# Spreading the routing pieces of a fused attention and mixture-of-experts kernel over three slots, with one-hots on GpSimd

## The chip, the cores and the metric

The kernel runs on one core of a Trainium2 chip. The time is that of one execution on the device, in microseconds (us); of several runs the median is given. Beside the runs there is one execution with the hardware profiler, whose span and instruction times the profile shows.

A core has five engines, each with its own queue of instructions, taken in order: TensorE (PE in the profile, with its weight loads as PEld), VectorE (DVE), ScalarE (ACT), GpSimd (POOL) and SyncE (SP, which here issues DMAs).

## The reference

```
scores = scale * q @ k.T              # 8 batches x 8 heads, 576 tokens, head_dim 64
scores masked in blocks of 64         # block_i >= block_j
x = softmax(scores) @ v               # -> x[b, s, 512]
logits = x @ w_gate                   # 8 experts
local_gate = sigmoid(x @ w_local)
for s:                                # within a batch
    fresh_e = argmax(logits[s])
    e = fresh_e if s == 0 or local_gate[s] < 0.5 else prev_e
    prev_e = e
    p = softmax(logits[s])
    out[s] = p[e] * (relu(x[s] @ w1[e]) @ w2[e])
```

So a token either takes the expert of its own largest logit or that of the token before it. The 4608 tokens are then sorted by expert into tiles of 128 rows, and each tile goes through the two matrices of one expert.

## The kernel before

The attention runs over 32 pairs of heads (`NPR`), in a loop over `it` from -2 to 31; one value of `it` is called a pass here. It is a pipeline by hand: in pass `it` the pair `a = it + 2` is transposed and begun, the pair `c = it + 1` gets its row maxima and its first scores, the pair `e = it` its last scores and its products with V (`av`), and the pair `x = it - 1` is written out as rows. The order of the instructions in each engine's queue is the order of the code (`manual_schedule`).

In one pass VectorE does, in this order: `norm` (L533, L534) of the pair before, the middle reduction to maxima (`mid_maxima`: L577, L581), the high reduction (`high_maxima`: the widest L577, then small copies and L599), the low reduction (`top(a, 2)`: L577, L579) and `norm_last` (L541 to L544). GpSimd does the exchange of maxima (L590 to L592) after the middle reduction and after the low one, the shift of the middle maxima (L599), casts of q and k (L992, L1032 to L1036), the clearing of corners (L651), the cast of x to bfloat16 (L505, in the last passes L510) and, in most passes, two loads of expert weights (L63), which it issues as DMAs. Score tiles in PSUM rotate over three buffers (`seg_tile`), so the scores of the high reduction reuse the buffer that the middle reduction has read. The gate's sums over four pairs (`gate_sums`, L732) come at the end of every fourth pass.

The tokens are routed in four groups of 9 columns of 128 tokens (`GC = 9`). The pieces of the routing of the first three groups are put into the passes by a table: `at(pass, slot, piece)` files a piece, and `run(pass, slot)` emits it at the named place of the pass. The slots that matter, in the order of a pass:

- start: after `norm`, ahead of the middle reduction
- mid: after the middle reduction and exchange, ahead of the last scores of `e` and the high reduction
- top, begin: after the high reduction
- turn: after the low exchange and the transposes of the gate's sums, ahead of the second weight load
- gap: behind that load, ahead of the last products `av(e, g1, 4)`, `av(e, g1, 3)` and of `norm_last`
- late: behind `norm_last`, ahead of the other products
- end, first: at the end of the pass

For group `g` the pieces begin in pass `i0` = 9, 17 and 26: `gate` (GpSimd, L159 to L163) and `fresh` in `i0`, `fresh_b` and the transposes `rows_ps` (L186) in `i0 + 1`, `scan_rows` (L192, L193) in `i0 + 2`, `carry` in `i0 + 3`, `scanned` and `chosen_ps` in `i0 + 4`, `chosen`, `ranks_ps` and the shares in `i0 + 5`, `ranks` and `ranks_all` in `i0 + 6`, `ranks_b` in `i0 + 7`, then `shares_b` (the share of a token as a sum of three bfloat16 parts) and `shares_out`, a DMA on SyncE. Two groups make the first 11 tiles of the expert stage; for these, `whole`, `whole_b`, `tile_experts`, `taken`, `taken_b`, `high` and `inverse` make the list of tokens, in passes 23 to 30. `low1(g, z)` makes the one-hots of the tokens' low rank bits, five or four columns of 128 at a time, in one VectorE instruction (L366); they are the left operand of `inverse`. In pass 30 the first rows are gathered. After pass 31 the expert stage runs over 36 tiles and more, with the fourth group's routing between them (`steps`).

Of the kernel before, what the change touches and what calls it, by code (L numbers as in the profile page):

```python
# [16 lines left out]
def kernel(  # L17
# [11 lines left out]
    nc = tc.nc  # L29
# [4 lines left out]
    AX = mybir.AxisListType.X  # L34
    AF = mybir.ActivationFunctionType
    ALU = mybir.AluOpType
# [6 lines left out]
    E = moe_w_gate.shape[1]  # L43
    F = moe_w1.shape[2]
    BS = B * S
    P = 128
# [24 lines left out]
    GC = BS // P // NG  # L71
# [8 lines left out]
    NTA = 2 * GC - E + 1  # L80
# [21 lines left out]
    desc_e = rt([P, E], F32, "desc_e")  # L102
# [4 lines left out]
    iota_lo = rt([P, P], BF16, "iota_lo")  # L107
# [11 lines left out]
    oh = rt([P, E, NC_], BF16, "oh")  # L119
# [35 lines left out]
    tmp = {}  # L155
# [9 lines left out]
    def fresh(g):  # L165

        lv = lg[:, :, :E]
        mx = sm9[:, 0, :]
        nc.vector.reduce_max(mx, lv, axis=AX)
        mxb = mx[:, :, None].to_broadcast([P, GC, E])  # L170
        nc.vector.tensor_tensor(tmp["eq"], lv, mxb, op=ALU.is_ge)
        nc.vector.tensor_sub(ep9, lv, mxb)
        nc.scalar.activation(ep9, ep9, func=AF.Exp)

    def fresh_b(g):
        best = sm9[:, 1, :]
        nc.vector.tensor_mul(tmp["eq"], tmp["eq"], desc_e[:, None, :].to_broadcast([P, GC, E]))
        nc.vector.reduce_max(best, tmp["eq"], axis=AX)
# [10 lines left out]
    def scan_rows(buf):  # L189

        s, kp = buf["sp"][:, 0, :], buf["sp"][:, 1, :]
        nc.vector.tensor_tensor_scan(s, kp, s, 0.0, op0=ALU.mult, op1=ALU.add)  # L192
        nc.vector.tensor_tensor_scan(buf["sp"][:, 1, :], kp, zeros, 1.0, op0=ALU.mult, op1=ALU.add)  # L193
        nc.vector.memset(buf["carry"][:, 0:1], 0.0)
# [35 lines left out]
    def ohg(g):  # L230
        return oh[:, :, GC * g:GC * g + GC]
# [30 lines left out]
    def ranks_all(g):  # L262
        off = sm9[:, 4, 0:E]
        nc.vector.tensor_add(tmp["pf"], tmp["pf"], off[:, :, None].to_broadcast([P, E, GC]))
        nc.vector.tensor_add(tmp["pf"], tmp["pf"], tots[:, 0, :].rearrange("p (e c) -> p e c", c=GC))
        nc.vector.tensor_mul(tmp["pf"], tmp["pf"], ohg(g))

    def ranks_b(g):
        rk = sm9[:, 5, :]
        nc.vector.reduce_sum(rk, over_e(tmp["pf"]), axis=AX)  # L270
        nc.vector.tensor_copy(ints[:, 0, 0, :], rk)
        nc.vector.tensor_single_scalar(ints[:, 1, 0, :], ints[:, 0, 0, :], 7,
                                       op=ALU.arith_shift_right)
        nc.vector.tensor_single_scalar(ints[:, 1, 1, :], ints[:, 0, 0, :], P - 1,
                                       op=ALU.bitwise_and)
        nc.vector.tensor_copy(hl[:, :, GC * g:GC * g + GC], ints[:, 1])
# [9 lines left out]
        nc.vector.reduce_sum(pg, ep9, axis=AX)  # L286
        nc.vector.tensor_mul(pgs, pg, sm)

    def shares_b(g):
        for j in range(3):  # L290
            nc.vector.tensor_copy(sh[:, :, j], pgs)
            if j < 2:
                nc.vector.tensor_sub(pgs, pgs, sh[:, :, j])

    def shares_out(g):
        nc.sync.dma_start(
            out=x_dram[GC * P * g:GC * P * g + GC * P, Dm:XW].rearrange("(c p) j -> p c j", p=P),
            in_=sh)

    def per_token(dst, w, n, tmp):  # L300

        nc.vector.tensor_mul(tmp, oh[:, :, 0:n], w[:, :, None].to_broadcast([P, E, n]))
        nc.vector.reduce_sum(dst, over_e(tmp), axis=AX)

    def shift7(dst, src, add):

# [120 lines left out]
    with tc.manual_schedule():  # L427
# [447 lines left out]
        def at(it, where, f):  # L875
            plan.setdefault((it, where), []).append(f)

        def low1(g, z):
            c0, n = GC * g + 5 * z, 5 - z
            low(ohl01[:, c0:c0 + n, :], c0, n)  # L880

        at(29, "first", lambda ps: inverse(ps, None, rhsa, na, NTA))
        for g in range(3):
            i0 = 8 * g + 9 + g // 2
            at(i0, "turn", lambda ps, g=g: gate(g))
            at(i0, "late" if g == 2 else "gap", lambda ps, g=g: fresh(g))
            at(i0 + 1, "gap", lambda ps, g=g: fresh_b(g))
            at(i0 + 1, "first", lambda ps: rows_ps(ps, buf))
            at(i0 + 2, "gap", lambda ps: scan_rows(buf))
            at(i0 + 2, "first", lambda ps: ends_ps(ps, buf))  # L890
            at(i0 + 2, "first", lambda ps: plan.update(ends=ends_in(ps)))
            at(i0 + 3, "gap", lambda ps: carry(plan["ends"], buf))
            at(i0 + 3, "first", lambda ps: carry_ps(ps, buf))
            at(i0 + 3, "first", lambda ps: carried(ps))
            at(i0 + 4, "gap", lambda ps: scanned(buf))
            at(i0 + 4, "first", lambda ps, g=g: chosen_ps(g, ps, buf))
            at(i0 + 4, "first", lambda ps: chosen_in(ps, nc.scalar.copy))
            at(i0 + 5, "start" if g == 2 else "gap", lambda ps, g=g: chosen(g))
            at(i0 + 5, "turned" if g == 2 else "first", lambda ps, g=g: ranks_ps(g, ps))
            at(i0 + 5, "turned" if g == 2 else "first", lambda ps: ranks_in(ps, nc.scalar.copy))  # L900
            if g == 2:
                at(i0 + 5, "gap", lambda ps, g=g: ranks(g))
                at(i0 + 5, "gap", lambda ps, g=g: ranks_all(g))
                at(i0 + 5, "end", lambda ps, g=g: ranks_b(g))
                break
            at(i0 + 5, "gap", lambda ps, g=g: shares_a(g))
            at(i0 + 5, "late", lambda ps, g=g: shares(g))
            at(i0 + 6, "gap", lambda ps, g=g: ranks(g))
            at(i0 + 6, "late", lambda ps, g=g: ranks_all(g))
            at(i0 + 7, "gap", lambda ps, g=g: ranks_b(g))  # L910
            at(i0 + 8 if g else i0 + 7, "late", lambda ps, g=g: shares_b(g))
            at(i0 + 9, "top", lambda ps, g=g: shares_out(g))
        at(17, "late", lambda ps: low1(0, 0))
        at(18, "late", lambda ps: low1(0, 1))
        at(23, "late", lambda ps: whole(False))
        at(24, "late", lambda ps: whole_b(NTA))
        at(25, "gap", lambda ps: tile_experts(tea, tend, NTA, tmpta))
        at(26, "gap", lambda ps: taken(t1ka, hia, na, tmpa))
        at(27, "late", lambda ps: taken_b(t1ka, hia, na))
        at(28, "turn", lambda ps: low1(1, 0))  # L920
        at(28, "late", lambda ps: high(ohha, rhsa, hia, 0, na, NTA))
        at(28, "late", lambda ps: high_b(ohha, rhsa))
        at(29, "gap", lambda ps: low1(1, 1))
        at(30, "start", lambda ps: inverse_in(plan["late"], inva, NTA))
        at(30, "mid", lambda ps: slots(inva, toka, None))
        for t in range(XGB):
# [312 lines left out]
        def highb():  # L1239
# [15 lines left out]
                 4: [lambda: shares_b(2), lambda: low2(0)],  # L1255
                 5: [lambda: shares_out(2), highb, lambda: gate(last), lambda: fresh(last)],
                 6: [lambda: inverse_in(cur[2], invb, NTB), lambda: slots(invb, tokb, None),
                     lambda: fresh_b(last)],
# [4 lines left out]
                 9: [lambda: chosen_in(cur[2], dve), lambda: chosen(last),  # L1263
                     lambda: new_g(1, lambda ps: ranks_ps(last, ps)),
                     lambda: ranks_in(cur[2], dve), lambda: ranks(last), lambda: ranks_all(last)],
                 10: [lambda: ranks_b(last), plan2],
# [93 lines left out]
```

## Time and profile before

| what | value |
|---|---|
| median of 3 runs | 458.43 us (458.36 to 460.65) |
| the profiled execution, its own time | 454.2 us |
| its span | 452.4 us |
| mean granted TensorE clock | 0.995 |
| TensorE busy | 432.8 us, 96% |
| VectorE busy | 315.1 us, 70% |
| GpSimd busy | 288.5 us, 64% |
| ScalarE busy | 273.6 us, 60% |

Busy time is the time in which an engine had an instruction in work. A row of a timeline gives the start, the length, the engine, the line of the kernel, the operation, what it writes and reads with shapes, a count, and in brackets the idle time before it with what ended that.

### The profile page before, as it was taken

What the parts mean: (1) busy time and instruction counts of PE and PEld (TensorE: products, weight loads), DVE (VectorE), ACT (ScalarE), POOL (GpSimd) and SP (SyncE); (2) the same over time, 40 slices, a digit from 0 to 9 for tenths busy, and PEclk for the clock granted to TensorE, in tenths of its full rate; (3) what the DMA queues carried; (4) which work ended last, traced back from release to release, by engine and by line L of the source; (5) the groups of instructions that cost most, each with busy time, mean ns of one, the idle gap of its engine ahead of it and who ended that gap; (6) DMA issues with size and microseconds to landing.
All of it is one profiled execution on the core that took longest, in us unless ns stands there. A gap on an engine that the chain in (4) does not pass through costs nothing.

```text
span 452.4 us, 19648 instructions
## 1 busy us (share of the span) xinstructions
PE 432.8 (96%) x7738; PEld 338.2 (75%) x7738; DVE 315.1 (70%) x856; ACT 273.6 (60%) x573; POOL 288.5 (64%) x674
## 2 busy tenths in 40 slices
PE   7899999999999999999999999987999999999994
PEld 5688787787788877787878777776676777777772
DVE  4777667768778888887788897954876884333422
ACT  3857766766667657665766666554454555555552
POOL 4556566667566747675556665672777758878853
PEclk8999999999999999999999999999999999999999
DMA  8999699999999975999779898887655665546532
GB/s 152 190 164 188 143 173 164 195 186 171 185 181 175 186 162 117 203 161 183 158 143 184 149 179 152 146 139 104 146 137 153 137 147 149 151 130 167 141 116 80
DMA packets 169885, 71.15 MB, mean 157 GB/s; under 512 B 151424, under 2 KB 158080, under 8 KB 169792
## 3 DMA queue, kind: packets, MB, share of 16 engines
q1 hardware_dynamic: 154640, 38.05, 44.5%
q0 software_dynamic: 13952, 31.52, 34.4%
q8 instruction: 64, 1.05, 1.0%
q10 hardware_dynamic: 1200, 0.30, 0.3%
q14 instruction: 29, 0.24, 0.2%
HBM read 67.18 MB, written 14.97 MB: 182 GB/s over the span
## 4 chain that ended last, share of the span: by engine, by line
PE 41%; DVE 26%; POOL 12%; issue 11%; DMA 5%; ACT 2%; POOLq 1%; DVEq 0%; ACTq 0%
PE g L667 10%; DVE mx L577 9%; PE ps_s L625 8%; POOL out_dram L822 6%; PE ps_s L634 4%; PE ps_h L798 4%; DMA out_dram<-o_sb,tok2s 3%; PE g L659 3%; PE ps_m L558 3%; PE ps_o L813 3%; PE g L951 2%; PE g L732 2%; DVE diag L599 2%; POOL diag L599 1%; DMA x_rows<-w_bf 1%
## 5 line engine op out<-in xcount | busy, mean ns | idle before, releaser
L641 ACT ACTIVATE prob<-ps_s 128x640 f32<-128x640 f32 (+2 forms) x128 | 103.6, 839 | 41.3 <-PE ps_s L634 40.4
L577 DVE TENSOR_REDUCE mx<-ps_m 128x2 f32<-128x640 f32 (+2 forms) x96 | 100.2, 1044 | 26.9 <-PE ps_m L558 19.9
L625 PE MATMUL ps_s<-plb 64*128 64x320 f32 (+4 forms) x768 | 107.3, 400 | 0.7 <-DVE mx L579 0.7
L625 PEld LDWEIGHTS ps_s<-plb 64*128 64x128 f32 x768 | 68.0, 189 | 20.8 <-issue 9.8
L667 PE MATMUL g<-vt,prob 128*64 128x65 f32 x2560 | 80.3, 222 | 0.0
L667 PEld LDWEIGHTS g<-vt,prob 128*64 128x64 f32 x2560 | 77.5, 138 | 0.1
L813 PE MATMUL ps_o<-w_bf,hT 128*128 x304 | 71.5, 380 | 0.0
L802 ACT ACTIVATE hT<-ps_h 128x512 bf16<-128x512 f32 x76 | 45.4, 597 | 26.6 <-PE ps_h L798 26.2
L816 ACT ACTIVATE o_sb<-ps_o,share 128x512 f32<-128x512 f32 x37 | 25.4, 686 | 40.2 <-PE ps_o L813 35.7
L813 PEld LDWEIGHTS <-hT 128*128 128x128 bf16 x304 | 28.0, 98 | 27.8 <-issue 0.3
L590 POOL COPY mx<-mx 64x2 f32<-64x2 f32 x64 | 11.7, 183 | 52.3 <-DVE mx L581 49.7
L779 DVE COPY natb<-w_bf 128x4096 bf16 x20 | 24.7, 1235 | 27.5 <-PE ps_h L798 25.2
L779 DVE COPY plb<-w_bf 128x4096 bf16 x20 | 25.1, 1253 | 24.6 <-PE ps_h L798 24.1
L798 PEld LDWEIGHTS <-plb 128*128 128x128 bf16 x608 | 35.4, 98 | 6.8 <-issue 2.9
L798 PEld LDWEIGHTS <-natb 128*128 128x128 bf16 x608 | 35.4, 98 | 6.2 <-DVE rs L541 1.5
L558 PE MATMUL ps_m<-kh,qh 64*128 64x320 bf16 (+3 forms) x256 | 37.6, 324 | 2.5 <-DVE mx L581 1.4
L634 PE MATMUL ps_s<-diag,ones 64*128 64x448 bf16 (+1 forms) x372 | 36.8, 274 | 2.0 <-DVE diag L599 0.4
L822 POOL DMA_INDIRECT out_dram<-o_sb,tok2s x17 | 28.7, 1690 | 11.6 <-ACT o_sb L816 7.0
L63 POOL DMA_DIRECT2D w_bf<-in_moe_w_dram x56 | 33.4, 596 | 1.4 <-DMA x_rows<-xb 0.4
L987 ACT COPY plb<-g 128x512 f32<-128x512 f32 x62 | 33.2, 593 | 0.3 <-PE g L951 0.2
L651 POOL MEMSET prob<- 64x128 f32 x128 | 24.5, 206 | 11.1 <-ACT prob L641 5.0
L798 PE MATMUL ps_h<-scr,plb 128*128 128x128 bf16 x416 | 25.3, 219 | 2.6 <-DVE share L788 2.3
(285 smaller groups left out, 769.8 us busy)
## 6 DMA issues: line engine op xcount, KB each, us to landing
w_bf<-in_moe_w_dram POOLq DMA_DIRECT2D x48, 256.0 KB, 4.5
vt<-in_v_dram SPq DMA_DIRECT2D x64, 128.0 KB
natb<-in_k_dram SPq DMA_DIRECT2D x63, 128.0 KB
natb<-in_q_dram SPq DMA_DIRECT2D x63, 128.0 KB
w_bf<-in_moe_w_dram POOLq DMA_DIRECT2D x8, 512.0 KB, 5.5
x_rows<-w_bf SPq DMA_DIRECT2D x13, 256.0 KB
natb<-in_k_dram SPq DMA_DIRECT2D x32, 32.0 KB
vt<-in_v_dram SPq DMA_DIRECT2D x32, 32.0 KB
```

The lines of the kernel that those rows point to most:

```text
L63: nc.gpsimd.dma_start(out=dst[:, e * WE:(e + 1) * WE].rearrange("p (k f) -> p k f", k=n)[:, r:r + m, :], in_=view[e][:, r:r + m, :])
L558: nc.tensor.matmul(ps[:, h, c:c + w], lhsT=qh[rows(h), 64 * b:64 * b + 128], rhs=kh[rows(h), 0:w], start=True, stop=m is None)
L577: nc.vector.reduce_max(mx[:, b:b + 2], ps[:, :, 0:w], axis=AX)
L625: nc.tensor.matmul(ps[:, h, c:c + n], lhsT=pls[i][rows(h), S + 128 * j:S + 128 * j + 128], rhs=pls[i][rows(h), a:a + n], start=part == 0, ...
L634: nc.tensor.matmul(ps[:, h, c:c + n], lhsT=ones[rows(h), :], rhs=diag[rows(h), a // 64:(a + n) // 64, :], start=False, stop=part == len(SE ...
L641: nc.scalar.activation(p[:, :, SEG0[s]:SEG0[s] + w], ps[:, :, 0:w], func=AF.Exp, scale=scale_attn)
L667: nc.tensor.matmul(g[rows(e), o + 65 * h:o + 65 * h + 65], lhsT=p[:, h, c:c + 64], rhs=t[:, j, h, :], start=(j == 0), stop=(j == m))
L779: nc.vector.tensor_copy(w, w1_bf[:, bass.ds(off, WE)])
L798: nc.tensor.matmul(ps_h[:, f, :], lhsT=w[:, f0 + ko * F:f0 + ko * F + 2 * P - 1:2], rhs=xb[:, ko * P:(ko + 1) * P], start=(ko == 0), stop= ...
L802: nc.scalar.activation(hT[:, half * 4:half * 4 + 4, :], ps_h, func=AF.Relu)
L813: nc.tensor.matmul(ps_o, lhsT=hT[:, fo, :], rhs=w2_bf[:, bass.ds(woff + fo * Dm, Dm)], start=(fo == 0), stop=(fo == FO - 1))
L822: wr = nc.gpsimd.indirect_dma_start(out=out_flat, out_offset=bass.IndirectOffsetOnAxis(ap=g[1][:, g[3]:g[3] + 1], axis=0), in_=o_sb, in_of ...
```

## The change

Pieces are cut in two and put elsewhere, and two kinds of work change the engine:

- `fresh_b` gives its first two instructions (L177, L178) to `fresh_a`, which goes to mid for the first two groups and to gap for the third. For the third group `fresh` goes from late to gap and `scan_rows` from gap to mid.
- `ranks_all` gives its last product (L266) to `ranks_own`, in mid of pass `i0 + 7`; `ranks_b` gives its first two instructions (L270, L271) to `ranks_a`, in gap; what is left of `ranks_b` goes to late, for group 1 one pass later than before.
- `shares_b` of the first two groups runs on GpSimd.
- `low1` runs on GpSimd, as one tensor_scalar for each column. For group 0 it stays late in passes 17 and 18; for group 1 it moves from turn of pass 28 and gap of pass 29 to late of passes 26 and 27.
- `whole` moves from late of pass 23 to gap of pass 24, `tile_experts` from gap to mid of pass 25. `taken` is cut into its two products (mid of passes 26 and 27) and its two reductions (late of the same passes); `taken_b` moves from late of pass 27 to gap of pass 28.
- In the expert stage the cut pieces run in the order that they had.

```
+    def fresh_a(g):
+        nc.vector.tensor_mul(tmp["eq"], tmp["eq"], desc_e[:, None, :].to_broadcast([P, GC, E]))
+        nc.vector.reduce_max(sm9[:, 1, :], tmp["eq"], axis=AX)
...
+    def ranks_own(g):
         nc.vector.tensor_mul(tmp["pf"], tmp["pf"], ohg(g))
 
-    def ranks_b(g):
+    def ranks_a(g):
         rk = sm9[:, 5, :]
         nc.vector.reduce_sum(rk, over_e(tmp["pf"]), axis=AX)
         nc.vector.tensor_copy(ints[:, 0, 0, :], rk)
+
+    def ranks_b(g):
...
-    def shares_b(g):
+    def shares_b(g, eng=nc.vector):
         for j in range(3):
-            nc.vector.tensor_copy(sh[:, :, j], pgs)
+            eng.tensor_copy(sh[:, :, j], pgs)
             if j < 2:
-                nc.vector.tensor_sub(pgs, pgs, sh[:, :, j])
+                eng.tensor_tensor(pgs, pgs, sh[:, :, j], op=ALU.subtract)
...
+    def per_token_a(w, n, tmp):
+        nc.vector.tensor_mul(tmp, oh[:, :, 0:n], w[:, :, None].to_broadcast([P, E, n]))
+
+    def per_token_b(dst, tmp):
+        nc.vector.reduce_sum(dst, over_e(tmp), axis=AX)
...
         def low1(g, z):
             c0, n = GC * g + 5 * z, 5 - z
-            low(ohl01[:, c0:c0 + n, :], c0, n)
+            for c in range(c0, c0 + n):
+                nc.gpsimd.tensor_scalar(ohl01[:, c, :], iota_lo, hl[:, 1, c:c + 1], 0.0,
+                                        op0=ALU.is_equal, op1=ALU.add)
...
-            at(i0, "late" if g == 2 else "gap", lambda ps, g=g: fresh(g))
+            at(i0, "gap", lambda ps, g=g: fresh(g))
+            at(i0 + 1, "gap" if g == 2 else "mid", lambda ps, g=g: fresh_a(g))
             at(i0 + 1, "gap", lambda ps, g=g: fresh_b(g))
             at(i0 + 1, "first", lambda ps: rows_ps(ps, buf))
-            at(i0 + 2, "gap", lambda ps: scan_rows(buf))
+            at(i0 + 2, "mid" if g == 2 else "gap", lambda ps: scan_rows(buf))
...
             at(i0 + 6, "late", lambda ps, g=g: ranks_all(g))
-            at(i0 + 7, "gap", lambda ps, g=g: ranks_b(g))
-            at(i0 + 8 if g else i0 + 7, "late", lambda ps, g=g: shares_b(g))
+            at(i0 + 7, "mid", lambda ps, g=g: ranks_own(g))
+            at(i0 + 8 if g else i0 + 7, "gap", lambda ps, g=g: ranks_a(g))
+            at(i0 + 8 if g else i0 + 7, "late", lambda ps, g=g: ranks_b(g))
+            at(i0 + 8 if g else i0 + 7, "late", lambda ps, g=g: shares_b(g, nc.gpsimd))
             at(i0 + 9, "top", lambda ps, g=g: shares_out(g))
         at(17, "late", lambda ps: low1(0, 0))
         at(18, "late", lambda ps: low1(0, 1))
-        at(23, "late", lambda ps: whole(False))
+        at(24, "gap", lambda ps: whole(False))
         at(24, "late", lambda ps: whole_b(NTA))
-        at(25, "gap", lambda ps: tile_experts(tea, tend, NTA, tmpta))
-        at(26, "gap", lambda ps: taken(t1ka, hia, na, tmpa))
-        at(27, "late", lambda ps: taken_b(t1ka, hia, na))
-        at(28, "turn", lambda ps: low1(1, 0))
+        at(25, "mid", lambda ps: tile_experts(tea, tend, NTA, tmpta))
+        at(26, "mid", lambda ps: per_token_a(t1, na, tmpa))
+        at(26, "late", lambda ps: per_token_b(t1ka, tmpa))
+        at(26, "late", lambda ps: low1(1, 0))
+        at(27, "mid", lambda ps: per_token_a(dd, na, tmpa))
+        at(27, "late", lambda ps: per_token_b(hia, tmpa))
+        at(27, "late", lambda ps: low1(1, 1))
+        at(28, "gap", lambda ps: taken_b(t1ka, hia, na))
         at(28, "late", lambda ps: high(ohha, rhsa, hia, 0, na, NTA))
         at(28, "late", lambda ps: high_b(ohha, rhsa))
-        at(29, "gap", lambda ps: low1(1, 1))
```

More of the change, by code (lines that the diff above doesn't have):

```diff
@@ L173, in fresh @@
         nc.scalar.activation(ep9, ep9, func=AF.Exp)
+    def fresh_a(g):
+        nc.vector.tensor_mul(tmp["eq"], tmp["eq"], desc_e[:, None, :].to_broadcast([P, GC, E]))
+        nc.vector.reduce_max(sm9[:, 1, :], tmp["eq"], axis=AX)
     def fresh_b(g):
         best = sm9[:, 1, :]
-        nc.vector.tensor_mul(tmp["eq"], tmp["eq"], desc_e[:, None, :].to_broadcast([P, GC, E]))
-        nc.vector.reduce_max(best, tmp["eq"], axis=AX)
         nc.vector.tensor_scalar(best, best, -1.0, float(E), op0=ALU.mult, op1=ALU.add)
@@ L298, in shares_out @@
             in_=sh)
+    def per_token_a(w, n, tmp):
+        nc.vector.tensor_mul(tmp, oh[:, :, 0:n], w[:, :, None].to_broadcast([P, E, n]))
+    def per_token_b(dst, tmp):
+        nc.vector.reduce_sum(dst, over_e(tmp), axis=AX)
     def per_token(dst, w, n, tmp):
-        nc.vector.tensor_mul(tmp, oh[:, :, 0:n], w[:, :, None].to_broadcast([P, E, n]))
-        nc.vector.reduce_sum(dst, over_e(tmp), axis=AX)
+        per_token_a(w, n, tmp)
+        per_token_b(dst, tmp)
     def shift7(dst, src, add):
@@ L903 @@
                 at(i0 + 5, "gap", lambda ps, g=g: ranks_all(g))
+                at(i0 + 5, "gap", lambda ps, g=g: ranks_own(g))
+                at(i0 + 5, "end", lambda ps, g=g: ranks_a(g))
                 at(i0 + 5, "end", lambda ps, g=g: ranks_b(g))
@@ L1257 @@
                  6: [lambda: inverse_in(cur[2], invb, NTB), lambda: slots(invb, tokb, None),
-                     lambda: fresh_b(last)],
+                     lambda: fresh_a(last), lambda: fresh_b(last)],
                  7: [lambda: scan_rows(buf)],
@@ L1264 @@
                      lambda: new_g(1, lambda ps: ranks_ps(last, ps)),
-                     lambda: ranks_in(cur[2], dve), lambda: ranks(last), lambda: ranks_all(last)],
-                 10: [lambda: ranks_b(last), plan2],
+                     lambda: ranks_in(cur[2], dve), lambda: ranks(last), lambda: ranks_all(last),
+                     lambda: ranks_own(last)],
+                 10: [lambda: ranks_a(last), lambda: ranks_b(last), plan2],
                  11: [plan2_a, lambda: plan2_b(tmp2, hi2)],
```

## The prediction

> **What bounds the kernel now.** I read the page first, then the chain of work that ended last, then the timelines of VectorE (DVE), GpSimd (POOL) and TensorE (PE), pass by pass. The page:
>
> ```profile
> span 452.4 us, 19648 instructions
> PE 432.8 (96%) x7738; PEld 338.2 (75%) x7738; DVE 315.1 (70%) x856; ACT 273.6 (60%) x573; POOL 288.5 (64%) x674
> PE 41%; DVE 26%; POOL 12%; issue 11%; DMA 5%; ACT 2%; POOLq 1%; DVEq 0%; ACTq 0%
> ```
>
> No engine bounds it alone: the chain changes hands inside each pass. Pass 7 holds no routing piece. Two pieces of its chain (start, length, what), then rows of the timelines of the three engines, picked out:
>
> ```profile
> 81.48 0.59 PE ps_s L634 x8
> ...
> 85.16 0.30 PE ps_m L558 x2
> ```
>
> ```profile
> 78.32 0.28 DVE L581 TENSOR_REDUCE mx<-ps_m 128x2 f32<-128x128 f32 x1
> 79.13 1.23 DVE L577 TENSOR_REDUCE mx<-ps_m 128x2 f32<-128x1024 f32 x1 [0.54 <-PE ps_m L558]
> 83.88 0.18 DVE L541 RECIPROCAL rs<-g 128x3 f32<-128x3 f32 x1 [1.11 <-PE g L667]
> 78.73 0.18 POOL L590 COPY mx<-mx 64x2 f32<-64x2 f32 x1 [1.40 <-DVE mx L581]
> 80.27 0.60 POOL L992 CAST qh<-plb 128x512 bf16<-128x512 f32 x1
> 80.98 0.30 PE L558 MATMUL ps_m<-kh,qh 64*128 64x320 bf16 x2
> ```
>
> I mark a pass by its widest reduction (L577 over 128x1024), which is always on the chain. From it to TensorE's L634 are 2.35 us (81.48 - 79.13), to the end of the last product with V 6.03 (85.16 - 79.13), and 2.57 more to the next mark, which stands at 87.73 (its row is the first below): a plain pass is 8.60 us.
>
> VectorE has idle time in two places: 0.54 us before the mark ("mid") and 1.11 before norm_last ("gap"). It has none after norm_last ("late"): the next instructions are L533 and L534, then the middle reduction, and TensorE's scores for the mark wait for that reduction to free their bank. GpSimd's exchange (L590) starts 0.13 us after the middle reduction; its chain ends with L992 at 80.87, 0.11 before the scores that read qh. So a delay of the middle reduction, or of GpSimd at that point, lengthens the pass almost at once.
>
> Where the routing lies, the marks are farther apart. The marks of passes 8, 9, 10 and 11, of 15 to 18, and of 23 to 29, each row alone out of VectorE's timeline:
>
> ```profile
> 87.73 1.23 DVE L577 TENSOR_REDUCE mx<-ps_m 128x2 f32<-128x1024 f32 x1 [0.54 <-PE ps_m L558]
> 97.54 1.23 DVE L577 TENSOR_REDUCE mx<-ps_m 128x2 f32<-128x1024 f32 x1 [0.85 <-PE ps_m L558]
> 106.13 1.23 DVE L577 TENSOR_REDUCE mx<-ps_m 128x2 f32<-128x1024 f32 x1 [0.53 <-PE ps_m L558]
> 115.48 1.23 DVE L577 TENSOR_REDUCE mx<-ps_m 128x2 f32<-128x1024 f32 x1 [0.85 <-PE ps_m L558]
> ```
>
> ```profile
> 151.85 1.23 DVE L577 TENSOR_REDUCE mx<-ps_m 128x2 f32<-128x1024 f32 x1 [0.67 <-PE ps_m L558]
> 160.97 1.23 DVE L577 TENSOR_REDUCE mx<-ps_m 128x2 f32<-128x1024 f32 x1 [0.49 <-PE ps_m L558]
> 170.79 1.23 DVE L577 TENSOR_REDUCE mx<-ps_m 128x2 f32<-128x1024 f32 x1 [0.85 <-PE ps_m L558]
> 179.70 1.23 DVE L577 TENSOR_REDUCE mx<-ps_m 128x2 f32<-128x1024 f32 x1 [0.49 <-PE ps_m L558]
> ```
>
> ```profile
> 224.77 1.23 DVE L577 TENSOR_REDUCE mx<-ps_m 128x2 f32<-128x1024 f32 x1 [0.71 <-PE ps_m L558]
> 234.36 1.23 DVE L577 TENSOR_REDUCE mx<-ps_m 128x2 f32<-128x1024 f32 x1 [0.49 <-PE ps_m L558]
> 244.45 1.23 DVE L577 TENSOR_REDUCE mx<-ps_m 128x2 f32<-128x1024 f32 x1 [0.85 <-PE ps_m L558]
> 253.88 1.23 DVE L577 TENSOR_REDUCE mx<-ps_m 128x2 f32<-128x1024 f32 x1 [0.49 <-PE ps_m L558]
> 262.98 1.23 DVE L577 TENSOR_REDUCE mx<-ps_m 128x2 f32<-128x1024 f32 x1 [0.49 <-PE ps_m L558]
> 271.92 1.23 DVE L577 TENSOR_REDUCE mx<-ps_m 128x2 f32<-128x1024 f32 x1 [0.49 <-PE ps_m L558]
> 282.50 1.23 DVE L577 TENSOR_REDUCE mx<-ps_m 128x2 f32<-128x1024 f32 x1 [0.85 <-PE ps_m L558]
> ```
>
> An idle time of 0.49 before a mark means that VectorE came last, since 0.49 is what TensorE takes after the middle reduction. A pass whose end holds gate_sums is 9.81 (87.73 to 97.54); every fourth is of that kind, 8, 16, 24 and 28 among those shown. Above 8.60 or 9.81 the passes that the change touches lose: pass 10 0.75, 15 0.52, 17 0.31, 23 0.99, 24 0.28, 25 0.83, 26 0.50, 27 0.34, 28 0.77. That is 5.29 us, and no more than that is to be had here. Pass 16 loses 0.01; in pass 18 I count no gain.
>
> **The change part by part.** The rows for the prices:
>
> ```profile
> 109.86 1.24 DVE L177 TENSOR_TENSOR scr<-scr,desc_e 128x72 f32<-128x72 f32 x1
> 110.28 0.72 POOL L505 CAST w_bf<-x 128x640 bf16<-128x640 f32 x1
> 185.72 0.32 PE g L186 x2
> 231.26 0.23 DVE L266 TENSOR_TENSOR scr<-scr,oh 128x72 f32<-128x72 f32 x1
> 231.41 0.17 DVE L308 TENSOR_SCALAR ints<-base 128x8 int32<-128x8 f32 x1
> 231.90 0.19 DVE L533 RECIPROCAL rs<-g 128x6 f32<-128x6 f32 x1
> 250.49 0.18 DVE L291 CAST sh<-pgs 128x9 bf16<-128x9 f32 x1
> 251.42 0.19 DVE L533 RECIPROCAL rs<-g 128x6 f32<-128x6 f32 x1
> 119.03 0.40 DVE L192 TENSOR_TENSOR_SCAN scr<-scr 9x128 f32<-9x128 f32 x1
> ```
>
> *Pass 10, fresh_a from gap to mid.* L177 took 1.24 us there, though its like (L266, same shape) takes 0.23: it ended 0.10 after GpSimd's cast L505 did, so it was held by that. In mid it and L178 (taken like L266) need some 0.5 us and have 0.53. The two instructions left in gap fit. Only the transposes of the next step stay on TensorE's path, 0.32: gain 0.75 - 0.32 = 0.43.
>
> *Pass 15, ranks_own out of late.* One L266 less, with its gap 0.26 us; it goes to mid of pass 16, where 0.49 are idle. Gain 0.26.
>
> *Pass 23, ranks_own and whole out of late.* From L308 to L533 were 0.49 us, L266 adds what remains from its start, 0.15: gain 0.64. They land in mid and gap of pass 24, the latter in place of ranks_b.
>
> *Pass 24.* ranks_b (five instructions, its second held by L505) leaves gap; three of whole come. whole_b stays in late, but norm_last is earlier, and gate_sums waited for it. This pass has the 1.21 us of gate_sums to hide whole_b. Gain 0.28.
>
> *Pass 25, late.* shares_b (0.93 us from 250.49 to 251.42) goes to GpSimd; three instructions of ranks_b, some 0.5 us, take its place, and tile_experts goes from gap to mid, where 0.85 are idle before 244.45. norm_last can then be about half a us earlier, as much as ranks_b needs. I take 0.78 of the 0.83.
>
> *Pass 27.* The reduction per_token_b replaces taken_b in late, but 0.32 of the loss of 0.34 is again the transposes: nothing.
>
> *Pass 28.* The first group's one-hots leave "turn", taken_b comes into gap, and two scans move from gap to mid. The scans need 0.40 each, 0.87 with what is around them; idle in mid are 0.49 and the 0.32 in which TensorE transposes. norm_last, for which gate_sums waited, is earlier: I take half of 0.77, 0.38, and 0 to 0.77 as bounds. The first scan also holds L590 up to 0.3 us, which is in these bounds.
>
> *Pass 29.* One one-hot piece leaves gap; the mark of pass 30 waits for other things by then: 0, at most +0.3.
>
> The sum of these is 0.43 + 0.26 + 0.64 + 0.28 + 0.78 + 0.38 = 2.77 us. The moved SP transfer, shares_out, keeps its pass; it waits for GpSimd's parts, finished more than half a pass before.
>
> *The one-hots on GpSimd* go the other way. Late in passes 17, 18, 26 and 27 come 5, 4, 5 and 4 tensor_scalar over 128x128, after the weight load in GpSimd's queue and ahead of the next exchange. In passes 17 and 26 the gate is in front of them too:
>
> ```profile
> 260.17 0.27 POOL L159 TENSOR_SCALAR ak<-lg 128x9 f32<-128x9 f32 x1
> 260.80 0.20 POOL L163 TENSOR_SCALAR sm<-ak 128x9 f32<-128x9 f32 x1
> 261.02 0.60 POOL L63 DMA_DIRECT2D w_bf<-in_moe_w_dram  x1
> L1036 POOL CAST qh<-plb 128x128 bf16<-128x128 f32 x31 | 9.1, 293 | 0.0
> ```
>
> GpSimd is free at 261.62. Undelayed, the next mark comes at 253.88 + 8.60 = 262.48, the exchange 0.40 before (79.13 - 78.73), at 262.08. To this I add a slack of 0.20, between 0.11 (80.87 to 80.98) and the 0.50 from 80.98 to L634. So 0.66 us are free. No row has this instruction at this size. Its nearest, L1036, is a one-input operation over 128x128 in 0.29; from below, 0.20 (L163, 128x9); from above, L159 compares 9 elements in 0.07 more than L163, which would be 1.0 us over 128 if it grew by element: 1.2. I take 0.30, by the nearest shape: five are 1.50, and the exchange is 0.84 late. Pass 17 then loses 0.84 instead of 0.31, pass 26 0.84 instead of 0.50: -0.87. Passes 18 and 27 have no gate (0.85 us, 260.17 to 261.02), so 1.51 are free and four cost 1.20: hidden; without that cover each would lose what passes 1.51. shares_b's five small steps (0.20 each, by L163) are hidden likewise in pass 25, and in pass 16.
>
> *Mid and GpSimd.* Eight steps in mid start 0.1 us before the exchange. The row of L177 shows that these two engines hold each other up. A step of 0.23 would hold L590 by about 0.1, inside the slack of 0.20: I count 0. [...]
>
> Net: 2.77 - 0.87 = 1.90 us. The profiled execution, 454.2 us with a span of 452.4, would take 452.3; the median of the runs shown, 458.43, lies 4.23 above it, and I take the same difference off: 456.5 us. From the bounds (one-hots at 0.25 to 0.40, where passes 18 and 27 lose 0.09 each too, and pass 28 from 0 to 0.77) this case alone reaches from 455.6 to 458.1.
>
> **The rivals.** *The one-hots fit.* If they cost 0.20 each, or the slack is nearer 0.50, passes 17 and 26 lose some 0.3 each instead of 0.81 together: gain 2.77 + 0.21 = 2.98, time 455.4. For it speaks the 0.20 of L163, where 119 more elements may add little; against it, the 0.29 of L1036 and the full queue of these two passes.
>
> *GpSimd becomes the bound (slower).* The place is the exchange after late in passes 17, 18, 26 and 27; the price is 5p - 0.66 twice and 4p - 1.51 twice for p us each. The old losses of 0.81 and the gains of 2.77 are used up at p = 0.44; from 0.56 on it is over 2.3 us slower. At 0.8 the time is 458.43 + 14.40 - 4.34 - 3.58 = 464.9. For it: L159's extra 0.07 for a compare of 9 elements. Against: L159 reads with a stride, and the 0.29 of L1036. [...]
>
> *Mid isn't free.* The exchange is held by each mid step for its whole length: six steps of 0.23 to 0.30 and the scans of 0.8, each less a slack of 0.11: 6 x 0.15 + 0.69 = 1.6 us are lost again. Time 458.1. For it: L177's row; against it: short steps and a start before the exchange.
>
> **How the numbers follow.** A difference of 0.5% (2.3 us) is about what a measurement of this kernel can tell from none. My forecast has 0.38, the fitting one-hots 0.30, the bound on GpSimd 0.22, mid not free 0.10. Forecast and last rival are within 0.5%: 0.48; faster 0.30; slower 0.22. The range goes from 454.8 (the fitting case with pass 28's whole 0.77 and 0.3 in pass 29) to 461.0, which takes in one-hots up to about 0.58; it leaves out the dearer ones.
>
> **What would show it.** In the changed profile the marks of passes 10, 23 and 25 should stand 8.9, 8.95 and 8.65 us before the next; L177 should take 0.23; the tensor_scalar of the one-hots some 0.30, with no idle time before L590 in the passes 18 and 27 that follow them. If passes 17 and 26 are 8.9 or less, the slack was larger; if they are over 10, GpSimd's compare is dear. The prediction is wrong if the marks outside passes 10 to 29 move, or if mid steps make VectorE come last where TensorE did.

## The result, and the profile after

The changed kernel takes 465.12 us (median of 8 runs, 462.45 to 467.25) against 459.32 us (8 runs, 456.35 to 460.65) for the kernel before beside it: ratio 1.0131, 95% interval 1.0101 to 1.0161. (Ratios, here and below, leave out runs over 1.5% above the fastest of the same kernel, and are not the quotients of the medians shown.) It is slower by 1.3%; forecast were 456.5 us and no more than 461.0. The profiled execution took 464.19 us.

Lines have moved in the changed kernel: the marks are L588 now, the middle reduction's end L592, the exchange L601, the cast of q L1013, the products with V L678; the one-hots on GpSimd are L892. The page's span, and in the same form as in the prediction the marks of passes 18 and 19, of 25, 26, 27 and 28:

```profile
span 462.5 us, 19661 instructions
```

```profile
180.59 1.23 DVE L588 TENSOR_REDUCE mx<-ps_m 128x2 f32<-128x1024 f32 x1
194.01 1.23 DVE L588 TENSOR_REDUCE mx<-ps_m 128x2 f32<-128x1024 f32 x1 [0.85 <-PE ps_m L569]
...
248.86 1.23 DVE L588 TENSOR_REDUCE mx<-ps_m 128x2 f32<-128x1024 f32 x1 [0.24 <-PE ps_m L569]
257.46 1.23 DVE L588 TENSOR_REDUCE mx<-ps_m 128x2 f32<-128x1024 f32 x1 [0.32 <-PE ps_m L569]
266.05 1.23 DVE L588 TENSOR_REDUCE mx<-ps_m 128x2 f32<-128x1024 f32 x1 [0.24 <-PE ps_m L569]
279.46 1.23 DVE L588 TENSOR_REDUCE mx<-ps_m 128x2 f32<-128x1024 f32 x1
```

Passes 25 and 26 are plain now: 8.60 and 8.59, where 9.43 and 9.10 were before. Passes 18 and 27 are 13.42 and 13.41, where 8.90 and 8.94 were. The marks by pass, in us to the next one:

| pass | before | forecast | after |
|---|---|---|---|
| 10 | 9.35 | 8.92 | 8.90 |
| 15 | 9.12 | 8.86 | 8.86 |
| 17 | 8.91 | 9.44 | 8.59 |
| 18 | 8.90 | 8.90 | 13.42 |
| 23 | 9.59 | 8.95 | 8.86 |
| 24 | 10.09 | 9.81 | 9.82 |
| 25 | 9.43 | 8.65 | 8.60 |
| 26 | 9.10 | 9.44 | 8.59 |
| 27 | 8.94 | 8.94 | 13.41 |
| 28 | 10.58 | 10.20 | 10.14 |
| 29 | 9.27 | 9.27 | 8.89 |

From the mark of pass 10 to that of pass 30 are 190.32 us (108.17 to 298.49) against 185.64 (106.13 to 291.77): 4.68 more, made of 8.99 lost in passes 18 and 27 and 4.3 gained in the others. So nearly all of the plan came true, and two passes took it back twice over. Of the 4.3, 0.2 is pass 13, which the change doesn't touch and which differs as much between profiles of one code.

What happens in one of the two, picked from the timelines of VectorE, GpSimd and TensorE:

```profile
179.15 0.60 POOL L63 DMA_DIRECT2D w_bf<-in_moe_w_dram  x1
179.78 0.28 DVE L592 TENSOR_REDUCE mx<-ps_m 128x2 f32<-128x128 f32 x1
179.80 3.52 POOL L892 TENSOR_SCALAR ohl<-iota_lo,hl 128x128 bf16<-128x128 bf16 x5
183.38 0.18 POOL L601 COPY mx<-mx 64x2 f32<-64x2 f32 x1
184.97 0.60 POOL L1013 CAST qh<-plb 128x512 bf16<-128x512 f32 x1
185.63 0.31 PE L569 MATMUL ps_m<-kh,qh 64*128 64x320 bf16 x2 [3.03 <-POOL qh L1013]
187.26 3.88 PE L678 MATMUL g<-vt,prob 128*64 128x65 f32 x80
```

The five one-hots of pass 17 take 3.52 us, 0.70 each. The middle reduction of pass 18 ends at 180.06, so the exchange could start 0.13 later, at 180.19; it starts at 183.38, 3.19 late. The cast of q ends at 185.57, and TensorE, which needs it, has stood for 3.03 us. What follows is a second loss: the 80 products with V take 3.88 us. In the same pass before they took 2.50:

```profile
183.22 2.50 PE L667 MATMUL g<-vt,prob 128*64 128x65 f32 x80
```

Pass 27 has a stall of 3.03 us too, and 3.77 us for the products. The clock granted to TensorE in pass 18, from the view of busy time by stretches (start and end, length, busy us and count of PE, PEld, DVE, ACT and POOL, then the granted clock; the last two columns are on DMAs and don't matter here):

```profile
184.00:185.60 1.60, 0.00 (x0) 0.00 (x0) 1.06 (x3) 0.04 (x1) 1.49 (x3) 1.00 1.34 167
185.60:186.50 0.90, 0.87 (x18) 0.56 (x20) 0.38 (x1) 0.10 (x1) 0.80 (x5) 1.00 1.20 126
186.50:187.50 1.00, 1.00 (x26) 1.00 (x28) 1.00 (x3) 1.00 (x2) 0.99 (x3) 0.65 0.36 52
187.50:188.50 1.00, 1.00 (x24) 1.00 (x22) 0.53 (x2) 0.74 (x1) 0.73 (x4) 0.50 0.54 68
188.50:189.50 1.00, 1.00 (x24) 1.00 (x22) 0.18 (x1) 0.00 (x0) 0.83 (x5) 0.50 1.04 181
189.50:190.50 1.00, 1.00 (x28) 1.00 (x26) 0.49 (x3) 0.00 (x0) 0.92 (x2) 0.64 0.91 256
190.50:191.50 1.00, 1.00 (x26) 0.71 (x24) 0.28 (x2) 0.01 (x1) 1.00 (x3) 1.00 0.94 133
```

Some 1.2 us after TensorE resumes at 185.63, the granted clock falls to 0.50, for some 3.4 us in which TensorE is busy all the time. Both times are estimates from the four stretches from 186.50 on (0.65 and 0.64 are means of stretches in which the clock changes).

### The profile page after: what moved, and what is told of

It reads as the page before. It is cut to its first block, busy times and chain, and to the rows that moved or that the text cites. A ratio compares the mean times of both kernels' runs of the same rounds, so it can differ in the third digit from the quotient of the medians.

```text
span 462.5 us, 19661 instructions
## 1 busy us (share of the span) xinstructions
PE 437.5 (95%) x7738; PEld 341.8 (74%) x7738; DVE 309.8 (67%) x842; ACT 271.4 (59%) x573; POOL 297.3 (64%) x702
## 4 chain that ended last, share of the span: by engine, by line
PE 62%; DVE 16%; POOL 6%; DMA 6%; issue 4%; ACT 3%; SPq 1%; another core or an unknown queue 1%; POOLq 0%; DVEq 0%; ACTq 0%
PE g L678 13%; PE ps_h L809 12%; PE ps_o L824 11%; PE ps_s L636 7%; DVE mx L588 6%; PE g L670 4%; PE ps_s L645 4%; PE ps_m L569 3%; DMA natb<-in_q_dram 2%; PE g L743 2%; PE g L972 2%; DMA x_rows<-w_bf 2%; DMA vt<-in_v_dram 2%; ACT prob L652 2%; POOL ohl L892 1%
## 5 line engine op out<-in xcount | busy, mean ns | idle before, releaser
L588 DVE TENSOR_REDUCE mx<-ps_m 128x2 f32<-128x640 f32 (+2 forms) x96 | 100.2, 1044 | 26.1 <-PE ps_m L569 16.7
L636 PE MATMUL ps_s<-plb 64*128 64x320 f32 (+4 forms) x768 | 106.1, 397 | 1.3 <-DVE mx L590 0.9
L678 PE MATMUL g<-vt,prob 128*64 128x65 f32 x2560 | 84.0, 226 | 0.5 <-issue 0.4
L678 PEld LDWEIGHTS g<-vt,prob 128*64 128x64 f32 x2560 | 80.8, 142 | 1.0 <-issue 0.9
L813 ACT ACTIVATE hT<-ps_h 128x512 bf16<-128x512 f32 x76 | 44.1, 597 | 47.7 <-PE ps_h L809 25.9
L601 POOL COPY mx<-mx 64x2 f32<-64x2 f32 x64 | 11.8, 185 | 43.4 <-DVE mx L592 37.1
L833 POOL DMA_INDIRECT out_dram<-o_sb,tok2s x17 | 21.6, 1270 | 18.4 <-ACT o_sb L827 9.5
```

Of the source, the lines that this page charges most:

```text
L588: nc.vector.reduce_max(mx[:, b:b + 2], ps[:, :, 0:w], axis=AX)
L636: nc.tensor.matmul(ps[:, h, c:c + n], lhsT=pls[i][rows(h), S + 128 * j:S + 128 * j + 128], rhs=pls[i][rows(h), a:a + n], start=part == 0, ...
L678: nc.tensor.matmul(g[rows(e), o + 65 * h:o + 65 * h + 65], lhsT=p[:, h, c:c + 64], rhs=t[:, j, h, :], start=(j == 0), stop=(j == m))
L813: nc.scalar.activation(hT[:, half * 4:half * 4 + 4, :], ps_h, func=AF.Relu)
```

## The experiments

My theory from here on (A): the one-hots on GpSimd cost all of the loss, by the late exchange and by the lower clock that follows the stall, and the rest of the change gains. Its rival (B): the steps in mid, and those that VectorE takes while GpSimd works, cost a part, so that the change is no faster without the one-hots.

**One-hots back on VectorE, all else as changed.**

```
-            for c in range(c0, c0 + n):
-                nc.gpsimd.tensor_scalar(ohl01[:, c, :], iota_lo, hl[:, 1, c:c + 1], 0.0, ...)
+            low(ohl01[:, c0:c0 + n, :], c0, n)
...
-        at(26, "late", lambda ps: low1(1, 0))
-        at(27, "late", lambda ps: low1(1, 1))
+        at(28, "turn", lambda ps: low1(1, 0))
+        at(29, "gap", lambda ps: low1(1, 1))
```

> The changed kernel with the one-hots of the first two groups on VectorE again, in the slots that they had before; all else as changed. Theory A (the one-hots on GpSimd cost all of the loss, by a late exchange, a stall of TensorE and a lower clock after it; the rest of the change gains): about 2.8 us less than before, some 456.5 against 459.3, passes 18 and 27 back to about 8.9. [...]

Measured: 453.82 us (10 runs) against 456.77 for the kernel before; ratio 0.9921, interval 0.9884 to 0.9958. The marks of pass 18 and 19:

```profile
183.94 1.23 DVE L588 TENSOR_REDUCE mx<-ps_m 128x2 f32<-128x1024 f32 x1
192.85 1.23 DVE L588 TENSOR_REDUCE mx<-ps_m 128x2 f32<-128x1024 f32 x1 [0.83 <-PE ps_m L569]
```

Pass 18 is 8.91 again, and passes 10 to 29 together are 182.91 us, 2.73 less than before. The expectation was 2.8. B has fallen: without the one-hots the change is faster than the kernel before. Whether mid costs a part is asked again below.

**One-hots on GpSimd alone, in the kernel before.**

```
-            low(ohl01[:, c0:c0 + n, :], c0, n)
+            for c in range(c0, c0 + n):
+                nc.gpsimd.tensor_scalar(ohl01[:, c, :], iota_lo, hl[:, 1, c:c + 1], 0.0, ...)
```

(and the same two pieces from passes 28 and 29 to late of 26 and 27)

> The kernel before with one part of the change alone: the one-hots as single instructions on GpSimd, late in passes 17, 18, 26 and 27. Theory A: about 8 us slower than before (two passes longer by 4.5 us each, less about 1 us that VectorE saves in passes 17, 28 and 29), ratio about 1.017, more than the whole change. Theory B: less than the whole change, under 1.010.

Measured: 462.89 us, ratio 1.0154 (1.0058 to 1.0251; 4 runs). Passes 10 to 29 take 192.02 us, 6.4 more than before, more than in the whole change (4.7) as A has it; but under the 8 expected, as pass 18 was only 11.80. The times alone can't tell 1.0154 from the whole change's 1.0131; this rests on the marks. Both stalls of this profile, and the clock after each:

```profile
186.30 0.31 PE L558 MATMUL ps_m<-kh,qh 64*128 64x320 bf16 x2 [2.98 <-POOL qh L994]
...
272.61 0.31 PE L558 MATMUL ps_m<-kh,qh 64*128 64x320 bf16 x2 [2.62 <-POOL qh L994]
```

```profile
188.00:189.00 1.00, 1.00 (x42) 1.00 (x38) 0.93 (x4) 0.91 (x2) 0.72 (x3) 1.00 0.55 70
...
274.50:275.50 1.00, 1.00 (x24) 1.00 (x22) 0.90 (x4) 0.72 (x1) 0.68 (x4) 0.50 0.74 101
```

A stall of 2.98 us left the clock at 1.00, one of 2.62 us halved it. In the first the products with V took 2.50 us, in the second 3.80. So the length of the stall alone doesn't decide.

**Three one-hots a pass**, in passes 17 to 19 and 26 to 28.

```
-            c0, n = GC * g + 5 * z, 5 - z
+            c0, n = GC * g + 3 * z, 3
...
+        at(19, "late", lambda ps: low1(0, 2))
+        at(28, "late", lambda ps: low1(1, 2))
```

> The changed kernel with three one-hots a pass in passes 17, 18, 19, 26, 27 and 28 instead of five and four. The exchange after passes 17 and 26 would be about 1.8 us late instead of 3.2, and TensorE would stand about 1.6 us instead of 3.0. If the lower clock comes only after a long stall (theory A1): TensorE's products with V take 2.33 us again and passes 18 and 27 are about 10.7 long; about 5.5 us less than the changed kernel, ratio to before 1.000. If any stall lowers the clock (A2): passes 18 and 27 about 12 us, ratio about 1.007.

Measured: 455.63 us, ratio 0.9947 (0.9903 to 0.9991). Passes 18 and 27 are 10.42 and 10.43. The stall and the products behind it:

```profile
186.13 0.31 PE L569 MATMUL ps_m<-kh,qh 64*128 64x320 bf16 x2 [1.61 <-POOL qh L1015]
...
187.55 2.50 PE L678 MATMUL g<-vt,prob 128*64 128x65 f32 x80
```

Half the stall, and the products take 2.50 us in this view, not 3.88; both stalls are 1.61 and neither lowers the clock (it stands at 1.00 in each stretch from 186.1 to 193.0). That is A1, for these two stalls. By the marks the kernel is level with before (185.59 us for passes 10 to 29, with 0.7 in pass 25 from a pause of TensorE that the experiment on the spread one-hots describes); the losses of 1.5 each in passes 18 and 27 eat most of the other gains. So the 0.5% by which its ratio is below 1.000 is more than the marks explain.

**The price of the one-hot by itself.** Sixteen more instructions on GpSimd ahead of the first pass:

```
+        for _ in range(2):
+            g.tensor_scalar(o1, iota_lo, n1, 0.0, op0=ALU.is_equal, op1=ALU.add)
+            g.tensor_scalar(o1, iota_lo, 5.0, 0.0, op0=ALU.is_equal, op1=ALU.add)
+            g.tensor_scalar(o1, iota_lo, n1, 0.0, op0=ALU.mult, op1=ALU.add)
+            g.tensor_scalar(o1, iota_lo, 5.0, 0.0, op0=ALU.mult, op1=ALU.add)
+            ... # the first and third in float32, then the first over 64 and 8 columns
```

> The kernel before with sixteen extra GpSimd instructions ahead of the first pass, whose results are overwritten later: tensor_scalar over 128 columns, compare or multiply, with the per-partition scalar or a constant, bfloat16 or float32, and the compare over 64 and 8 columns, each twice. The one-hot took 0.71 us in the changed kernel. If the compare is dear, the multiply takes 0.3 and the compare 0.7 in both types; if the scalar operand is dear, the constant takes 0.3; if bfloat16 is dear, float32 takes 0.3; if all tensor_scalar cost by element alike, all take 0.7 over 128, 0.45 over 64 and 0.2 over 8.

GpSimd's timeline in the one run of it, the second round:

```profile
7.68 0.71 POOL L859 TENSOR_SCALAR ohl<-iota_lo,nth 128x128 bf16<-128x128 bf16 x1
8.48 0.64 POOL L860 TENSOR_SCALAR ohl<-iota_lo 128x128 bf16<-128x128 bf16 x1
9.22 0.37 POOL L861 TENSOR_SCALAR ohl<-iota_lo,nth 128x128 bf16<-128x128 bf16 x1
9.68 0.30 POOL L862 TENSOR_SCALAR ohl<-iota_lo 128x128 bf16<-128x128 bf16 x1
10.05 0.71 POOL L863 TENSOR_SCALAR lgS<-id_f,nth 128x128 f32<-128x128 f32 x1
10.86 0.37 POOL L864 TENSOR_SCALAR lgS<-id_f,nth 128x128 f32<-128x128 f32 x1
11.20 0.50 POOL L865 TENSOR_SCALAR ohl<-iota_lo,nth 128x64 bf16<-128x64 bf16 x1
11.80 0.33 POOL L866 TENSOR_SCALAR ohl<-iota_lo,nth 128x8 bf16<-128x8 bf16 x1
```

The compare is what is dear: 0.71 against 0.37 for the multiply with the same operands. The scalar operand costs 0.07 of it (0.71 to 0.64, 0.37 to 0.30), the type nothing (float32 took 0.71 and 0.37 too). The compare grows by 3.2 ns a column ((0.71 - 0.33) / 120).

**TensorE kept busy through the stall.**

```
+            if job == 2 and i in (20, 29):
+                for _ in range(44):
+                    nc.tensor.matmul(ps[:, 0, 0:P], lhsT=ones, rhs=ones, start=True, stop=True)
             scores(ps, b, 0, w, m)
```

(`i` is the pair of heads: 20 and 29 are reached in passes 18 and 27.)

> The changed kernel with 44 extra small products on TensorE in passes 18 and 27, right before the scores that wait for the late cast; what they write is overwritten by these scores. They fill most of the stall and take nothing from the chain. Theory A1 (4.5 us a pass are 2.9 us of waiting and 1.5 us of products at a lower clock, which comes from the idle stretch): the clock stays at 1.0, the products with V take 2.33 us instead of 3.66, passes 18 and 27 are about 12.0 instead of 13.4; some 3 us less than the changed kernel. Rival (the low clock comes from what runs then, not from idleness): still 13.4.

Measured: 464.72 us against 460.21, ratio 1.0076 (1.0037 to 1.0115). The extra products (41 of the 44 stand in this row), the scores behind them, and the products with V (L681 here):

```profile
183.81 2.45 PE L579 MATMUL ps_m<-ones 128*128 128x128 bf16 x41
...
186.71 0.31 PE L569 MATMUL ps_m<-kh,qh 64*128 64x320 bf16 x2 [0.45 <-POOL qh L1016]
...
188.13 2.50 PE L681 MATMUL g<-vt,prob 128*64 128x65 f32 x80
```

```profile
188.00:190.50 2.50, 2.50 (x92) 2.50 (x86) 1.78 (x7) 1.31 (x2) 2.05 (x9) 1.00 0.89 117
```

The clock stays at 1.00 in both passes, and passes 18 and 27 are 11.83 and 11.84, by 44 products that do nothing for the result. This divides the loss: of the 4.5 us in each pass 2.92 are waiting (11.83 - 8.91) and 1.59 the clock (13.42 - 11.83). The same products run here at a clock of 1.00: the rival, that they bring the low clock, has fallen in these passes, and I put the low clock down to the idle stretch. The evidence is both filled stalls with the clock kept, against three of four unfilled ones of 2.6 to 3.0 us with it lost. Passes 19 and 28 are 9.25 and 10.74 here, 0.5 and 0.6 longer than in the changed kernel: the four one-hots that follow cost something once TensorE isn't slowed beside them. Altogether passes 10 to 29 are 188.53 us, 1.8 less than in the changed kernel and not the 3 expected.

**The shares' parts back on VectorE too** (first experiment's kernel, `shares_b(g)` for `shares_b(g, nc.gpsimd)`).

> The changed kernel with the one-hots and also the shares' parts (shares_b) on VectorE, as the first experiment but for the latter. Theory A: the pass in whose late slot they stand grows, as 0.9 us then lies behind 0.5 us of ranks_b: pass 25 from 8.60 to about 9.4, pass 16 unchanged since gate_sums covers it. Rival (GpSimd gains nothing there): pass 25 stays at 8.60.

One run. The marks of passes 25 and 26:

```profile
244.99 1.23 DVE L588 TENSOR_REDUCE mx<-ps_m 128x2 f32<-128x1024 f32 x1 [0.24 <-PE ps_m L569]
254.27 1.23 DVE L588 TENSOR_REDUCE mx<-ps_m 128x2 f32<-128x1024 f32 x1 [0.28 <-PE ps_m L569]
```

9.28 instead of 8.59, pass 16 unchanged at 9.82: GpSimd takes 0.69 us off pass 25.

**Mid emptied** (first experiment's kernel, all pieces of mid filed under gap of the same pass).

> The first experiment's kernel (one-hots on VectorE) with all pieces of mid put into gap of the same pass: fresh_a, ranks_own, tile_experts, the two products of per_token and the third group's scans. Theory A (mid is idle time, a step there costs nothing): passes 10 and 25 grow by 0.3 to 0.6 (to about 9.3 and 9.1), pass 26 by some 0.3. Rival C (steps in mid hold the exchange and cost as much as they save): these passes stay, and passes 16, 24 and 27 become shorter.

One run. The marks of passes 10 and 11:

```profile
109.44 1.23 DVE L588 TENSOR_REDUCE mx<-ps_m 128x2 f32<-128x1024 f32 x1 [0.54 <-PE ps_m L569]
118.79 1.23 DVE L588 TENSOR_REDUCE mx<-ps_m 128x2 f32<-128x1024 f32 x1 [0.85 <-PE ps_m L569]
```

Pass 10 is 9.35 as before the change (8.91 with mid); passes 24 to 28 grow by 0.26, 0.37, 0.09, 0.80 and 0.75. The 0.80 of pass 27 is not the edit's: its products with V hold a pause of 0.53 us that waits for nothing visible, and take 3.31 us instead of 2.50. Against the first experiment passes 15 and 16 are shorter, by 0.19 and 0.30, but they are 8.85 and 9.82 here as in the changed kernel (8.86 and 9.82), whose mid is filled: the first experiment's profile scatters there. Passes 10 to 29 are 185.14 us, 2.2 more than the first experiment's, some 1.4 without the pause. Passes 10 and 25 came out as expected (about 9.3 and 9.1), pass 26 grew less. Rival C has fallen: none of passes 16, 24 and 27 is shorter than where mid is filled. The changed kernel's own trace says the same: with a step in mid, the exchange starts 0.13 to 0.14 us after the middle reduction in passes 10, 16, 24 and 25, as in the plain pass 7 before, and passes 16, 24, 25 and 26 are as long as passes without routing. So these steps in mid cost nothing.

**The one-hots spread by GpSimd's room.**

```
+        for i, c0, n in ((18, 0, 2), (19, 2, 2), (20, 4, 3), (21, 7, 2), (27, 9, 2), (28, 11, 4)):
+            at(i, "late", lambda ps, c0=c0, n=n: low1(c0, n))
+        at(29, "gap", lambda ps: low(ohl01[:, 15:18, :], 15, 3))
```

> The changed kernel with the one-hots on GpSimd spread by the room that its idle time before the exchange shows: 2, 2, 3 and 2 late in passes 18 to 21, 2 and 4 late in passes 27 and 28, and the last three on VectorE in gap of pass 29. Theory A: no exchange is late, no stall of TensorE, passes 17, 18, 26, 27 and 28 at about 8.6, 8.95, 8.6, 8.9 and 10.15; some 4 us less than before in the passes, 1 us less than with the one-hots on VectorE, ratio about 0.990. [...]

By the marks it did what was expected: passes 17, 18, 26, 27 and 28 at 8.60, 8.91, 8.59, 8.91 and 10.12, passes 19 to 21 unchanged with two, three and two one-hots late in them (8.76, 9.93 and 8.70 in a second profile of this kernel, 8.76, 9.93 and 8.70 before), passes 10 to 29 in 181.48 us, 4.16 less than before. The time was 459.44 us against 460.21, ratio 0.9974 (0.9943 to 1.0004), so 3 us of the gain were missing. The profile shows TensorE pausing in the expert stage, where it waited for nothing visible, for instance

```profile
381.18 0.66 PE L809 MATMUL ps_h<-xb,natb 128*128 128x128 bf16 x9 [1.05 <-issue]
```

**The same again, and the kernel before itself, on one chip.**

> The kernel before, unchanged, for a second profile of it. In the profiles of the changed kernel and of some experiments TensorE pauses for about a microsecond at several tiles of the expert stage (that stage is 4 to 6 us longer there than in the profile of before), though its code is the same. If this belongs to the execution or the chip and not to the change, this profile has such pauses too, or its expert stage differs from the first profile's by some us; the marks of passes 10 to 29 stay within 0.2 us of the first profile's. If it belongs to the change, the expert stage is 160.6 us after the mark of pass 30 again, without pauses.

> The first experiment's kernel again (one-hots on VectorE), beside the spread one on one chip. By its marks it gains 2.7 us in passes 10 to 29: ratio 0.994. If the expert stage of the changed kernels is slower, the ratio is nearer to 1.

> The spread one-hots again, on the same chip as the kernel with one-hots on VectorE. By its marks it gains 4.2 us in passes 10 to 29, 1.4 more than that: ratio 0.991. It was 0.997 in the last measurement; if the marks are right and that was the chip's scatter, it comes out below the other one here; if not, something outside passes 10 to 29 takes the gain back, and it is at 0.997 again.

Of this second profile of the kernel before, the span and the mark of pass 30:

```profile
span 456.5 us, 19626 instructions
```

```profile
294.54 1.23 DVE L577 TENSOR_REDUCE mx<-ps_m 128x2 f32<-128x1024 f32 x1
```

Passes 10 to 29 took 185.61 us, 0.03 from the first profile, and the rest 162.0 instead of 160.6, without such pauses; but TensorE stood 2.50 us for a DMA there, and its clock was halved after it (last section). The spread kernel took 452.45 us against 456.07, ratio 0.9935 (0.9905 to 0.9965); passes 10 to 29 181.23 us, the expert stage 159.9 us where it had been 165.5, without pauses, from the same code. The kernel with one-hots on VectorE took 453.27 us, ratio 0.9926 (0.9895 to 0.9956). So the code doesn't fix the pauses: the same kernel ran once with them and once without. That the change has no part in them is not shown. Of the nine profiles of kernels made from the changed one eight hold at least one pause of this kind over 0.3 us, in the passes too (1.33 in pass 3 of the first experiment, 1.13 in pass 15 of its second profile); of the four of kernels made from the one before, none does. Their cause stays open. On this chip both versions beat the kernel before, and by their ratios to it the changed one too. Which of the two is faster the times can't tell (the intervals overlap). By the marks the spread one is 1.4 us shorter than the first profile of the other (181.48 to 182.91), and 2.8 shorter in the second profiles (181.23 to 184.01), where the other has the pause of 1.13.

## Why the prediction was wrong

Its view of the pass was right in the main, and the step that failed is one term, the price of a one-hot on GpSimd: "I take 0.30, by the nearest shape". The one-hot takes 0.71, so that the exchange was 3.19 us late where the forecast had 1.04 (0.84 and the slack of 0.20). A second term was missing, the clock after the stall (below). The nearest row, a cast over the same 128x128, is like the multiply with a constant (0.30), not like the compare. The row that pointed the right way was cited for the rival, L159 with its compare; its bound of 1.2 and the rival's point of 0.56 held the case, with a chance of 0.22.

*The rest of the formula held.* For a pass with the gate it gave 5p - 0.66: at 0.71 that is 2.89, and the experiment with TensorE kept busy measured 2.92. For three one-hots it gives 1.47; measured were 1.51 (10.42 - 8.91). Free room and slack were right to a few hundredths in the passes with the gate.

*The four one-hots* of passes 18 and 27 should have cost 4p - 1.51 = 1.33; in the changed kernel the exchange came on time (0.13 after the middle reduction in pass 19), since that reduction was itself late behind the slowed products; with the clock kept up the exchange of pass 19 was 1.10 late, and the two passes lost 0.5 and 0.6. That they were "hidden", as forecast, was luck.

*The clock is missing from the prediction.* 1.59 and 1.57 us in the two passes, 3.2 of the 9.0 lost, follow from the stall and not from the one-hots' length. With it the rival at p = 0.71 would have come to 8.9 us for the two passes (2 x (2.89 + 1.58)). Without it, the rival's formula gives 18 x 0.71 - 4.34 - 3.58 = 4.9 us slower, close to the 4.7 of the marks, but by two errors that cancel: 2.7 for the four one-hots, which didn't come, and nothing for the clock, 3.2.

*The place was one pass off.* The one-hots late in pass 17 delay the exchange of pass 18, which comes 0.4 before that pass's mark but is needed after it. The loss is in the pass after; 17 and 26 themselves lost their old 0.32 and 0.51.

*The gains* were 0.45, 0.26, 0.73, 0.27, 0.83 and 0.44 in passes 10, 15, 23, 24, 25 and 28, against 0.43, 0.26, 0.64, 0.28, 0.78 and 0.38: 2.98 against 2.77. Pass 29 gave 0.38, where 0 to 0.3 was stated (the sum of 5.29 us "to be had" leaves this pass out): without the one-hots in gap norm_last came earlier, it seems; no run takes that apart.

*The rival that mid isn't free* fell with the emptied mid. The step that took 1.24 us beside the cast in gap (L177, L176 now) takes 0.22 in mid of pass 10 and 0.29 in mid of pass 18, beside a one-hot on GpSimd; in gap of pass 27, where the third group has it, it takes 0.54 beside a cast (L521). So VectorE's step took longer where a cast was in work on GpSimd, though L177 started 0.42 us ahead of that cast; and L176 of pass 18 ended at 180.27, before the first one-hot did (about 180.50, at 0.70 each). That the two engines hold each other up, as the prediction has it, these rows show on VectorE's side alone: the cast L505 took 0.72 beside L177, and 0.73 in the median of its 26 in the kernel before.

*Outside passes 10 to 29* the profile of before was a short one: the rest of the 5.8 us between the medians beyond 4.7 can lie in stages of unchanged code, where the two profiles of the kernel before differ by as much (106.13 and 108.93 us to the mark of pass 10, 160.6 and 162.0 from that of pass 30). Which it is no run shows.

## What to carry to other kernels

Price an instruction by its operation first and by its shape second: on GpSimd a compare over 128 columns took 0.71 us here and a multiply 0.37. Ahead of a small step that others wait for, count the room from that step's row, as 0.66 us here, and spread the piece by it: five one-hots of 0.71 lengthened the pass by 2.92, which is all that they had over this room. If the engine that then waits is TensorE, allow for a lower clock behind the wait: here it followed five of seven stalls of 2.16 to 3.03 us and neither of two of 1.61, and cost 1.6 us in each of passes 18 and 27.

## What the runs showed of the hardware

Stalls of TensorE of 3.03, 3.03 and 2.62 us in the passes were followed by a granted clock of 0.50 for some 3.4 us, starting 1.0 to 1.2 us after work resumed; one of 2.98 us was not, nor were two of 1.61. In the expert stage, where the first tile waits for its rows, the traces hold three more, of the kernel before, of its second profile, and of the kernel with three one-hots a pass:

```profile
309.30 1.95 PE L798 MATMUL ps_h<-scr,plb 128*128 128x128 bf16 x32 [2.27 <-DVE share L788]
...
309.03 3.23 PE L798 MATMUL ps_h<-scr,natb 128*128 128x128 bf16 x31 [2.50 <-DMA scr<-scr]
...
312.13 2.63 PE L809 MATMUL ps_h<-scr,plb 128*128 128x128 bf16 x32 [2.16 <-DMA scr<-scr]
```

Behind 2.27 us the clock stayed at 1.00; behind 2.50 and 2.16 it was 0.50 for 3.4 us, from 0.4 and 1.1 us after work resumed, and the like products took 3.23 (31 of them) and 2.63 us against 1.95. The change has no part in the second of these. So between 2.16 and 3.03 us five stalls of seven were followed by half the clock, without order of length. Ahead of the first passes it was 0.50 for a like stretch without such a stall (from about 7.3 to 10.7 us in the kernel before, where the longest waits of TensorE until then were 1.14 and 0.61 us). What decides whether the clock falls these runs don't show.

Filling the stall with 44 extra products kept the clock at 1.00 in both passes, and the products with V took 2.50 us instead of 3.88; of the pass that took off 1.6 us (13.42 to 11.83).

GpSimd's compare took 0.71, 0.50 and 0.33 us over 128, 64 and 8 columns in bfloat16, which makes an estimated 3.2 ns a column and 0.3 us besides (float32 the same 0.71 over 128); its multiply took 0.37 us over 128.
